# Scaled upper words of 20 weight pieces in idle PSUM banks, all scaled on ScalarE: local attention and a rational FFN on one core

## The chip, the cores and the metric

The kernel runs on one core of a Trainium2 chip. A core has five engines with an instruction stream each: TensorE (PE: matrix products and transposes; PEld is its loading of weights), VectorE (DVE), ScalarE (ACT), GpSimd (POOL) and SyncE (SP, which here issues nearly all DMAs). SBUF is the working memory with 128 partitions; PSUM has eight banks of 2 KB per partition. Products land in PSUM. GpSimd works on SBUF alone here. The metric is the device time of one launch in microseconds, the median of several runs; lower is better.

## The reference: what is computed

Attention with a window of 96 keys and 8 global keys, over 4 batches, 8 heads, 768 positions and head size 64, then an FFN with a rational activation, 512 to 2048 to 512, over the 3072 tokens. Cut to what matters:

```python
scores = scale * np.matmul(q, k.transpose(0, 1, 3, 2))
keep = is_global | is_local
scores = np.where(keep, scores + bias, -1000000000.0)
a = np.exp(scores - np.max(scores, axis=-1, keepdims=True))
x = np.matmul(a / np.sum(a), v)          # as 3072 x 512
...
h = x @ w_in                              # 512 x 2048
P = a[0] + a[1] * h + a[2] * h2 + a[3] * h3
Q = 1.0 + np.abs(b[0]) * np.abs(h) + np.abs(b[1]) * h2
return ((P / (Q + 1e-06)) @ w_out).astype(np.float32)   # 2048 x 512
```

The two weight matrices arrive as 64-bit floating-point numbers. [...]

## The kernel before

**Tiling.** The 3072 tokens are cut into 12 chunks of 256 (`TOK`). A chunk has eight attention units (two blocks of 128 positions by four pairs of heads) and eight FFN blocks of 256 hidden columns. There are 96 of each. The loop of `windowed` (L592) goes through 111 steps `t`; in each it calls the stages of several units at different ages: scores of unit t−1, transposed probabilities of t−2, values of t−3, and FFN block f, which is t−10 for the first chunks (`turn`, L588).

**What sets the order.** Each stage is given a number (`cur_priority`, from the tables `PRI` and `PRI_A` and the step), and a scheduler that simulates the engines puts every engine's instructions in a fixed order by it. On the chip an engine works through its own order strictly and waits where an operand isn't ready. Tiles are taken from pools: tiles of one tag share a fixed number of buffers, and a new one waits until an earlier one is done with.

**PSUM.** Eight banks: two with the tag `h` (the first FFN product), two `acc` (the second product's sums), one `r` (1/Q, written by ACT on L323, read and overwritten by DVE on L327 to L329), and three `t` for attention. The FFN begins about ten steps after attention, so the five banks of `h`, `acc` and `r` hold nothing in the first steps.

**The first chunk** runs with plain 32-bit products (`h` on L274, `acc` on L353) straight from the decoded weights `full`. From the second chunk on each product is a sum of three with a high and a low part of the weights (L282, L358), which `split_w` (L231) makes.

**The weights.** There are 32 pieces of 128 rows by 512 numbers, 512 KB each as they arrive: 16 of `w_in` and 16 of `w_out`. `WSCHED` says at which step which pieces are decoded, two at a time: pieces 0 and 1 at step 0, 2 and 3 at step 1, then steps 3, 4, 6, 7, 8, 9, 10 and 11 up to pieces 18 and 19, and the last 12 at steps 12 to 16. `fetch` (L175) brings a piece into one of five raw buffers by a DMA on SP (L182). `decode` (L184) then works in four steps; `MODE` lists who does the first two (3 for piece 0, 5 for pieces 1, 3, 5, 7, 9, 11, 14, 17 and 20, 2 for the other 22):

- L211 or L213: the upper words, read as a 32-bit number, times 2 to the −112, into the piece's SBUF buffer `dst`: by POOL (mode 5) or by ACT, which takes the magnitude as well.
- L215 (POOL, or ACT on L217 for the first piece): the upper half of the lower word, scaled to three bits, in place in the raw buffer (`low`).
- L218 (DVE): the sign of the upper word joined to `low`, in place in the raw buffer. It needs no scaled upper word.
- L220 (DVE): the scaled upper word shifted left by three, joined to `low`, in `dst`.

All operands of L218 and L220 lie in SBUF. The raw buffer is free for the next fetch after L220.

**Others named below.** L463 is attention's mask and row extreme on DVE, L473 the exponentials on ACT, L476 a small sum after them on DVE, L544 the first chunk's attention output; L313, L314 and L327 to L329 are the FFN's operations on DVE, L315 its addition on POOL.

Of the kernel before, what the change touches and what calls it, by code (L numbers as in the profile page):

```python
# [9 lines left out]
F32 = mybir.dt.float32  # L10
FR = mybir.dt.float32r
I32 = mybir.dt.int32
BF16 = mybir.dt.bfloat16
U16 = mybir.dt.uint16
AF = mybir.ActivationFunctionType
ALU = mybir.AluOpType
PSUM = bass.MemoryType.PSUM

P = 128
# [3 lines left out]
FLOOR = -0.5 + 2.0 ** -14  # L23
# [16 lines left out]

SPLITS = {4: 0, 5: 2, 6: 4, 7: 8, 8: 12, 9: 16, 10: 19, 11: 22, 12: 25, 13: 28, 14: 32}

MODE = (3, 5, 2, 5, 2, 5, 2, 5, 2, 5, 2, 5, 2, 2, 5, 2, 2, 5, 2, 2, 5, 2, 2, 2, 2, 2, 2, 2, 2, 2, 2, 2)
HI_V = (0, 2, 4, 6, 8, 10, 12, 14, 16, 18, 20, 22, 24, 26, 28, 30)
LO_V = (13, 15, 17, 19, 21, 23, 25, 27, 29, 31)

# [59 lines left out]
def tile_kernel(ctx: ExitStack, tc: tile.TileContext, q, k, v, n_global, n_local,  # L106
                w_in, w_out, ca, cb, out):
    nc = tc.nc
# [5 lines left out]
    TOK = 2 * P  # L114
# [8 lines left out]
    pl = SimpleNamespace(tmps=TMPS, gbufs=GBUFS, split=False)  # L123
# [34 lines left out]
    full = {}  # L158
    hi = {}

    def piece(dt, key):
        return wide.tile([P, 2 * TOK], dt, tag="w", name=f"w{'_'.join(map(str, key))}{'f' if dt is F32 else 'h'}",
                         bufs=NCT * DF // (2 * TOK) + NFT + 1)
# [11 lines left out]
    def fetch(key, eng=nc.sync):  # L175
        z, r, j = (*key, 0)[0:3]
        r = slice(r * P, (r + 1) * P)
        src = w_in_i[r, 4 * j * TOK:4 * (j + 1) * TOK] if z else w_out_i[r, :]
        home = (pl.early, "raw", 2) if (len(full) + len(fetched)) % 5 in (1, 3) else (pl.ffn, "g", pl.gbufs)
        raw = home[0].tile([P, 2, 2, TOK], F32, tag=home[1], name="r" + "_".join(map(str, key)), bufs=home[2])  # L180
        raw = fetched[key] = raw.rearrange("p z a b -> p (z a b)").rearrange("p (f w) -> p f w", w=2)
        eng.dma_start(out=raw.bitcast(I32), in_=src.rearrange("p (f w) -> p f w", w=2))  # L182

    def decode(key):  # L184
        dst = full[key] = piece(F32, key)
        if key not in fetched:
            fetch(key)
        raw = fetched.pop(key)
        bits = dst.bitcast(I32)
        top, low = raw.bitcast(I32)[:, :, 1], raw.bitcast(I32)[:, :, 0]  # L190
        half = raw.bitcast(U16).rearrange("p f (w z) -> p f w z", z=2)[:, :, 0, 1]
        mode = MODE[len(full) - 1]
        if mode < 2:


            nc.scalar.activation(out=dst, in_=raw[:, :, 1], func=AF.Abs)
            guard = nc.gpsimd if mode else nc.vector
            guard.tensor_scalar(out=dst, in0=dst, scalar1=1.125 * 2.0 ** -15, scalar2=None, op0=ALU.max)
            nc.vector.tensor_scalar(out=bits, in0=bits, scalar1=3, scalar2=0x3FFFFFFF,
                                    op0=ALU.logical_shift_left, op1=ALU.bitwise_and)  # L200
            nc.vector.scalar_tensor_tensor(out=bits, in0=top, scalar=-0x40000000, in1=bits,
                                           op0=ALU.bitwise_and, op1=ALU.bitwise_or)
            nc.vector.scalar_tensor_tensor(out=bits, in0=low, scalar=29, in1=bits,
                                           op0=ALU.logical_shift_right, op1=ALU.bitwise_or)
            return

        if mode == 5:  # L210
            nc.gpsimd.tensor_scalar(out=dst, in0=raw[:, :, 1], scalar1=2.0 ** -112, scalar2=None, op0=ALU.mult)  # L211
        else:
            nc.scalar.activation(out=dst, in_=raw[:, :, 1], func=AF.Abs, scale=2.0 ** -112)  # L213
        if mode != 3:
            nc.gpsimd.tensor_scalar(out=low, in0=half, scalar1=2.0 ** -13, scalar2=FLOOR, op0=ALU.mult, op1=ALU.add)  # L215
        else:
            nc.scalar.activation(out=low, in_=half, func=AF.Copy, scale=2.0 ** -13, bias=FLOOR)  # L217
        nc.vector.scalar_tensor_tensor(out=low, in0=top, scalar=-0x80000000, in1=low,  # L218
                                       op0=ALU.bitwise_and, op1=ALU.bitwise_or)
        nc.vector.scalar_tensor_tensor(out=bits, in0=bits, scalar=3, in1=low,  # L220
                                       op0=ALU.logical_shift_left, op1=ALU.bitwise_or)

    w_in_i = w_in.bitcast(I32)
    w_out_i = w_out.bitcast(I32)
# [333 lines left out]
    def windowed(lates):  # L558
# [33 lines left out]
        for t in range(NU + LAG + F2 + 1):  # L592
# [75 lines left out]
            for n, (kind, j) in enumerate(WSCHED.get(t, ())):  # L668
                tc.cur_priority = base + 1000 * t + pri[False]["dec"] + 50 * n
                for key in pieces(kind, j):  # L670
                    decode(key)
# [162 lines left out]
```

## Time and profile before

| what | value |
|---|---|
| median of 3 runs | 759.34 us (757.77 to 762.38) |
| the profiled execution | 762.41 us, of which the recorded span is 760.6 us |
| mean granted TensorE clock | 0.993 |
| PE busy | 730.6 us, 96% of the span |
| DVE, ACT, POOL busy | 609.0, 577.6, 455.4 us |
| DMA | 62.17 MB, mean 82 GB/s |

A busy share over the whole run says little here, because the run has a start of about 100 us, in which weights arrive and are decoded while attention is already running, and a long even part after it. In forty equal slices of the span (19 us each) the tenths of busy time are:

```profile
PE   4788989999999999999999999999999999999996
DVE  5789985888798878888788878778888788886565
ACT  5687866986887877877877877877887878776764
POOL 4585665584666666746656656566466656665441
DMA  8876500204332322323322322233322331200000
```

PE is not full in the first five slices, and DMA is at its highest there. These are the slices in which the change lies; stretches cut to fit are shown with the prediction. In such lines the engines are told apart by column, a group's row gives its count, its busy time and mean, and then the idle time of the engine just before it with what ended that.

### The profile page before, as it was taken

Reading aid. Unit: us, or ns where it says so; the run is one execution under the profiler, and the core shown is the slowest. Engines: PE = TensorE matmul, PEld = TensorE weight load, DVE = VectorE, ACT = ScalarE, POOL = GpSimd, SP = SyncE. Lnnn points to the kernel's source line nnn. Section 1 sums busy time; section 2 is a strip of 40 time slices with the busy share of each in tenths; the row PEclk is TensorE's granted clock in tenths of the full one; section 3 lists DMA queues with packets and bytes.
Section 4 is the critical chain, followed back from the end, with each engine's and each line's share of the span. In section 5 each row is a group of like instructions: output and inputs, shape, how many; then the busy total and the mean of one; then the engine's idle time right before and its main releaser. Section 6 shows DMA issues by size and latency. Waiting matters only on the chain.

```text
span 760.6 us, 15061 instructions
## 1 busy us (share of the span) xinstructions
PE 730.6 (96%) x5072; PEld 635.3 (84%) x5072; DVE 609.0 (80%) x1440; ACT 577.6 (76%) x1302; POOL 455.4 (60%) x488
## 2 busy tenths in 40 slices
PE   4788989999999999999999999999999999999996
PEld 3566657788988988998999989988988988998995
DVE  5789985888798878888788878778888788886565
ACT  5687866986887877877877877877887878776764
POOL 4585665584666666746656656566466656665441
PEclk9999999999999999999999999999999999999999
DMA  8876500204332322323322322233322331200000
GB/s 232 254 245 181 185 22 15 57 22 111 91 79 69 104 64 58 101 64 74 101 53 58 101 61 66 84 78 77 89 59 64 90 72 37 71 16 1 28 1 33
DMA packets 111959, 62.17 MB, mean 82 GB/s; under 512 B 81664, under 2 KB 100096, under 8 KB 111872
## 3 DMA queue, kind: packets, MB, share of 16 engines
q1 hardware_dynamic: 111584, 61.11, 29.8%
q8 instruction: 42, 0.69, 0.4%
q14 instruction: 45, 0.37, 0.2%
q10 hardware_dynamic: 288, 0.00, 0.0%
HBM read 35.92 MB, written 6.29 MB: 55 GB/s over the span
## 4 chain that ended last, share of the span: by engine, by line
PE 87%; DVE 6%; DMA 2%; issue 2%; POOL 1%; ACT 1%; SPq 0%; DVEq 0%; POOLq 0%
PE h L282 34%; PE acc L358 33%; PE o L522 5%; PE tp L497 5%; PE s L449 4%; PE acc L353 3%; DVE r L218 2%; DMA r<-in_moe_w_in_dram 2%; PE s L444 1%; PE tk L394 1%; PE h L274 1%; DMA nat<-in_k_dram 1%; DVE pr L463 1%; PE o L513 0%; POOL r L215 0%
## 5 line engine op out<-in xcount | busy, mean ns | idle before, releaser
L487 POOL TENSOR_SCALAR pr<-pr,stats 128x256 f32<-128x256 f32 (+1 forms) x152 | 132.9, 885 | 108.8 <-DVE stats L478 64.5
L282 PE MATMUL h<-xh,win_l 128*128 128x256 f32 x704 | 197.5, 281 | 0.0
L315 POOL TENSOR_TENSOR fa<-fa,fs 128x512 f32<-128x512 f32 x95 | 125.1, 1317 | 83.2 <-ACT fs L308 73.2
L358 PE MATMUL acc<-wout_l,g 128*128 128x512 f32 x352 | 139.4, 396 | 0.0
L282 PEld LDWEIGHTS h<-xh,win_l 128*128 128x128 f32 x704 | 133.1, 189 | 2.0 <-issue 0.5
L338 POOL TENSOR_TENSOR g<-fu,g 128x512 fp32r<-128x512 f32 x87 | 113.9, 1309 | 32.0 <-ACT g L337 25.9
L473 ACT ACTIVATE pr<-pr,stats 128x256 f32<-128x256 f32 (+1 forms) x192 | 92.7, 485 | 30.8 <-DVE stats L463 28.9
L306 ACT ACTIVATE fu<-h,coef 128x512 f32<-128x512 f32 (+1 forms) x97 | 75.1, 774 | 27.8 <-PE h L282 23.9
L327 DVE SCALAR_TENSOR_TENSOR fu<-fu,coef,q 128x512 f32<-128x512 f32 (+1 forms) x97 | 71.7, 739 | 29.9 <-ACT q L323 27.3
L322 ACT ACTIVATE fs<-fa,coef 128x512 f32<-128x512 f32 (+1 forms) x97 | 69.5, 716 | 27.6 <-POOL fa L315 25.8
L313 DVE TENSOR_TENSOR fu<-fu,h 128x512 f32<-128x512 f32 (+1 forms) x97 | 65.5, 675 | 16.8 <-ACT fs L308 16.7
L358 PEld LDWEIGHTS acc<-wout_l,g 128*128 128x128 f32 x352 | 66.4, 189 | 9.6
L314 DVE SCALAR_TENSOR_TENSOR fu<-fu,coef,h 128x512 f32<-128x512 f32 (+1 forms) x97 | 71.7, 739 | 1.9
L427 DVE SCALAR_TENSOR_TENSOR kq<-tk,kq 64x256 fp32r<-64x256 f32 x144 | 60.8, 422 | 14.7 <-ACT kq L426 10.5
L328 DVE SCALAR_TENSOR_TENSOR q<-fa,coef,q 128x512 f32<-128x512 f32 (+1 forms) x97 | 72.1, 743 | 0.0
L499 DVE COPY pT<-tp 128x512 f32<-128x512 f32 (+1 forms) x75 | 48.4, 645 | 28.0 <-PE tp L497 26.9
L426 ACT ACTIVATE kq<-tk 64x256 fp32r<-64x256 f32 x144 | 54.3, 377 | 19.2 <-DVE kq L427 13.5
L308 ACT ACTIVATE fs<-h,coef 128x512 f32<-128x512 f32 (+1 forms) x97 | 66.3, 684 | 2.0 <-DMA out_dram<-o 1.8
L329 DVE SCALAR_TENSOR_TENSOR fu<-q,fu 128x512 f32<-128x512 f32 (+1 forms) x97 | 66.1, 681 | 1.6
L337 ACT CAST g<-fu 128x512 fp32r<-128x512 f32 (+1 forms) x89 | 54.8, 615 | 15.0 <-DVE fu L329 14.6
L307 ACT ACTIVATE fa<-h,coef 128x512 f32<-128x512 f32 (+1 forms) x97 | 65.6, 676 | 0.0
L497 PE MATMUL tp<-ident,pr 128*128 128x128 f32 x352 | 57.3, 275 | 2.5 <-DVE stats L463 2.4
(253 smaller groups left out, 2049.0 us busy)
## 6 DMA issues: line engine op xcount, KB each, us to landing
mv<-nat SPq DMA_DIRECT2D x36, 256.0 KB
qT<-kq SPq DMA_DIRECT2D x144, 64.0 KB
r<-in_moe_w_in_dram SPq DMA_DIRECT2D x16, 512.0 KB
r<-in_moe_w_out_dram SPq DMA_DIRECT2D x16, 512.0 KB
nat<-in_q_dram SPq DMA_DIRECT2D x48, 128.0 KB
nat<-in_k_dram SPq DMA_DIRECT2D x48, 128.0 KB
vt<-in_v_dram SPq DMA_DIRECT2D x48, 128.0 KB
out_dram<-o SPq DMA_DIRECT2D x24, 256.0 KB
```

The costliest lines, as they stand in the source:

```text
L282: nc.tensor.matmul(out=hps[f][:, y, :], lhsT=w[:, fs], rhs=x[:, ct, :], start=(n == 0), stop=(n == 3 * NCT - 1))
L306: nc.scalar.activation(out=u, in_=h, func=AF.Identity, scale=a3, bias=a2)
L314: nc.vector.scalar_tensor_tensor(out=u, in0=u, scalar=a1, in1=h, op0=ALU.add, op1=ALU.mult)
L315: side(f).tensor_tensor(out=a, in0=a, in1=s, op=ALU.add)
L322: nc.scalar.activation(out=s, in_=a, func=AF.Ln, bias=q1)
L327: nc.vector.scalar_tensor_tensor(out=u, in0=u, scalar=a0, in1=r, op0=ALU.add, op1=ALU.mult)
L328: nc.vector.scalar_tensor_tensor(out=r, in0=a, scalar=q1, in1=r, op0=ALU.add, op1=ALU.mult)
L338: side(f).tensor_tensor(out=g[:, 1, ys], in0=u, in1=g[:, 0, ys], op=ALU.subtract)
L358: nc.tensor.matmul(out=acc, lhsT=gs[f][:, z, y, ts], rhs=w, start=(ft == 0 and n == 0), stop=(ft == NFT - 1 and n == 2))
L473: nc.scalar.activation(out=d, in_=d, func=AF.Exp, scale=-1.0, bias=st[:, x:x + 1], accum_out=st[:, 2 + 2 * x:3 + 2 * x])
L487: nc.gpsimd.tensor_scalar(out=d, in0=d, scalar1=st[:, 6 + x:7 + x], scalar2=None, op0=ALU.mult)
L497: nc.tensor.transpose(out=t_ps[:, x, w, :], in_=pr[:, x, w, :], identity=ident)
```

## The change

For every piece ACT now scales the upper word and takes its magnitude (`mag`); POOL's version is gone, and so is the table `MODE` with a branch that no piece used. The lower word is scaled by ACT for piece 0 and by POOL for all others, as before. For pieces 0 to 19 `mag` lies in a PSUM tile, whose pool `BANKS` names by a letter: `h` for pieces 0, 2, 5 and 7, `r` for 1, 6, 10, 13, 16 and 19, `a` (tag `acc`) for the ten others. For pieces 20 to 31 it lies in `dst`, as before. The two DVE operations change places and operands: the first shifts `mag` and joins `low`, in place in `mag`; the second joins the sign of the raw upper word and writes `dst`. So the first now needs ACT's result. For the first 20 pieces each of the two reads one SBUF operand and one in PSUM; for the last 12 both operands stay in SBUF.

```diff
-MODE = (3, 5, 2, 5, 2, 5, 2, 5, 2, 5, 2, 5, 2, 2, 5, 2, 2, 5, 2, 2, 5, 2, 2, 2, 2, 2, 2, 2, 2, 2, 2, 2)
+LOW_A = (0,)
+BANKS = "hrhaa" * 2 + "raa" * 3 + "r" + " " * 12
...
-        bits = dst.bitcast(I32)
+        n = len(full) - 1
...
+        mag = dst
+        if BANKS[n] != " ":
+            pool, tag = dict(h=(pl.ps_h, "h"), r=(pl.ps_r, "r"), a=(pl.ps_o, "acc"))[BANKS[n]]
+            mag = pool.tile([P, 2 * TOK], F32, tag=tag, name=f"m{n}")
+        bits = mag.bitcast(I32)
...
-        if mode == 5:
-            nc.gpsimd.tensor_scalar(out=dst, in0=raw[:, :, 1], scalar1=2.0 ** -112, scalar2=None, op0=ALU.mult)
+        nc.scalar.activation(out=mag, in_=raw[:, :, 1], func=AF.Abs, scale=2.0 ** -112)
+        if n in LOW_A:
+            nc.scalar.activation(out=low, in_=half, func=AF.Copy, scale=2.0 ** -13, bias=FLOOR)
         else:
-            nc.scalar.activation(out=dst, in_=raw[:, :, 1], func=AF.Abs, scale=2.0 ** -112)
-        if mode != 3:
             nc.gpsimd.tensor_scalar(out=low, in0=half, scalar1=2.0 ** -13, scalar2=FLOOR, op0=ALU.mult, op1=ALU.add)
-        else:
-            nc.scalar.activation(out=low, in_=half, func=AF.Copy, scale=2.0 ** -13, bias=FLOOR)
-        nc.vector.scalar_tensor_tensor(out=low, in0=top, scalar=-0x80000000, in1=low,
-                                       op0=ALU.bitwise_and, op1=ALU.bitwise_or)
         nc.vector.scalar_tensor_tensor(out=bits, in0=bits, scalar=3, in1=low,
                                        op0=ALU.logical_shift_left, op1=ALU.bitwise_or)
+        nc.vector.scalar_tensor_tensor(out=dst.bitcast(I32), in0=top, scalar=-0x80000000, in1=bits,
+                                       op0=ALU.bitwise_and, op1=ALU.bitwise_or)
```

More of the change, by code (lines that the diff above doesn't have):

```diff
@@ L188, in decode @@
         raw = fetched.pop(key)
-        bits = dst.bitcast(I32)
+        n = len(full) - 1
         top, low = raw.bitcast(I32)[:, :, 1], raw.bitcast(I32)[:, :, 0]
         half = raw.bitcast(U16).rearrange("p f (w z) -> p f w z", z=2)[:, :, 0, 1]
[L192 to L201, printed above, removed]
-                                           op0=ALU.bitwise_and, op1=ALU.bitwise_or)
-            nc.vector.scalar_tensor_tensor(out=bits, in0=low, scalar=29, in1=bits,
-                                           op0=ALU.logical_shift_right, op1=ALU.bitwise_or)
-            return
@@ L215, in decode @@
+        nc.scalar.activation(out=mag, in_=raw[:, :, 1], func=AF.Abs, scale=2.0 ** -112)
+        if n in LOW_A:
+            nc.scalar.activation(out=low, in_=half, func=AF.Copy, scale=2.0 ** -13, bias=FLOOR)
+        else:
             nc.gpsimd.tensor_scalar(out=low, in0=half, scalar1=2.0 ** -13, scalar2=FLOOR, op0=ALU.mult, op1=ALU.add)
-        else:
-            nc.scalar.activation(out=low, in_=half, func=AF.Copy, scale=2.0 ** -13, bias=FLOOR)
-        nc.vector.scalar_tensor_tensor(out=low, in0=top, scalar=-0x80000000, in1=low,
-                                       op0=ALU.bitwise_and, op1=ALU.bitwise_or)
```

## The prediction

> **What bounds the kernel now.** I read the stretches of time first, since the change touches only the first seventh of the run. Columns: stretch, length, busy time of PE, PEld, DVE, ACT and POOL with instruction counts, granted PE clock, DMA share, GB/s. The last line is the page's span.
>
> ```profile
> 0.00:20.00 20.00, 10.21 (x45) 7.48 (x45) 11.05 (x53) 10.10 (x37) 9.26 (x22) 1.00 0.85 234
> 20.00:62.00 42.00, 33.05 (x215) 25.25 (x215) 35.47 (x92) 31.69 (x96) 31.29 (x33) 0.96 0.79 246
> 62.00:97.50 35.50, 31.11 (x161) 21.39 (x159) 35.50 (x67) 26.43 (x61) 19.37 (x21) 1.00 0.54 169
> 97.50:200.00 102.50, 102.49 (x634) 81.40 (x635) 80.84 (x188) 78.72 (x183) 65.43 (x62) 0.98 0.19 46
> 200.00:740.00 540.00, 540.00 (x3953) 488.68 (x3952) 434.92 (x1022) 422.40 (x911) 326.16 (x349) 1.00 0.26 66
> span 760.6 us, 15061 instructions
> ```
>
> From 97.5 us on PE never stops. So the weight decode, which ends near 100 us, can change the time in one way only: by the moment at which PE begins its unbroken run. PE's idle time before that is 42 − 33.05 = 8.95 us in 20 to 62 and 35.5 − 31.11 = 4.39 us in 62 to 97.5, 13.3 us together, and that is the most there is to win. In the second stretch DVE is busy all 35.5 us. The chain of waits (start, length, what) says the same: DMA until 20.50, then a mixture that is mostly DVE, then PE.
>
> ```profile
> 20.50 0.40 DVE x L544
> ...
> 85.62 1.68 DVE w_10f L220
> ...
> 96.85 0.61 DVE fu L329
> 97.51 5.40 PE acc L353 x8
> ```
>
> The timeline of PE shows what it waits for at its two long gaps, and that it then runs slower for a while: the pair of products that takes 1.02 us at 86.90 takes 1.91 us at 98.65.
>
> ```profile
> 58.39 3.72 PE L274 MATMUL h<-x,w_1f 128*128 128x256 f32 x16 [2.22 <-DVE fu L314]
> ...
> 86.90 1.02 PE L353 MATMUL acc<-w_4f,fu 128*128 128x512 f32 x2
> 97.51 1.35 PE L353 MATMUL acc<-w_6f,fu 128*128 128x512 f32 x2 [2.39 <-DVE fu L329]
> 98.65 1.91 PE L353 MATMUL acc<-w_7f,fu 128*128 128x512 f32 x2
> ```
>
> Both gaps end on DVE: it is late with the FFN because it also does two operations for each of 32 weight pieces (L218, L220). So the sum below is one of DVE's time between 20 and 97.5 us.
>
> **The change, part by part.**
>
> *POOL loses the nine upper-word scalings* (L211). Two of them lie before 20 us and seven between 20 and 62; the two lines are POOL's time for L211 in these stretches.
>
> ```profile
> 0.00:20.00 20.00, 3.25 (x2) 1.00 0.85 234
> 20.00:62.00 42.00, 12.22 (x7) 0.96 0.79 246
> ```
>
> POOL, busy 31.29 of 42 us there, drops to about 19. The two before 20 us I cost at nothing: there the chain stands on DMA, whose share is 0.85 and which no edit relieves. What the other seven are worth is what DVE pays for them now. DVE's group of L218 in 20 to 62 (busy and mean, then idle before it and its releaser) holds a direct wait for POOL, and both of its decode lines run longer than their own median. The line after it is the time of L220 in 20 to 62, the last two are L218 and L220 in 62 to 104.
>
> ```profile
> L218 DVE SCALAR_TENSOR_TENSOR r<-r 128x512 int32<-128x512 int32 x16 | 12.3, 771 | 2.3 <-POOL r L215 2.3
> 20.00:62.00 42.00, 12.69 (x15) 0.96 0.79 246
> 62.00:104.00 42.00, 11.83 (x13) 0.96 0.46 143
> 62.00:104.00 42.00, 12.63 (x14) 0.96 0.46 143
> ```
>
> *DVE's operands move to PSUM for 20 pieces.* The lengths of single instructions (minimum, median, maximum in ns) separate the kinds. L218 reads two SBUF operands; L329 reads one PSUM and one SBUF operand and has plain constants, as the new second operation does; L327 and L328 have a pointer scalar besides, and L328 also writes PSUM, as the new first operation does.
>
> ```profile
> L218 DVE SCALAR_TENSOR_TENSOR r<-r x32: 674/693/1753, 10.8 to 96.2; 128x512 int32<-128x512 int32 x32
> L327 DVE SCALAR_TENSOR_TENSOR fu<-fu,coef,q x97: 479/746/750, 61.7 to 750.3; 128x512 f32<-128x512 f32 x95, 128x256 f32<-128x256 f32 x2
> L328 DVE SCALAR_TENSOR_TENSOR q<-fa,coef,q x97: 480/748/754, 62.4 to 750.7; 128x512 f32<-128x512 f32 x95, 128x256 f32<-128x256 f32 x2
> L329 DVE SCALAR_TENSOR_TENSOR fu<-q,fu x97: 424/689/694, 64.7 to 751.2; 128x512 f32<-128x512 f32 x95, 128x256 f32<-128x256 f32 x2
> ```
>
> Two things follow. First, no operation with a PSUM operand is ever stretched, in 97 cases each and with POOL busy beside them, while the all-SBUF ones reach 1753 ns. One such stretch in the timeline: DVE starts while POOL is inside a two-operand addition and ends 0.55 us after it, which is most of its own 0.69 us.
>
> ```profile
> 52.89 1.58 POOL L315 TENSOR_TENSOR fa<-fa,fs 128x512 f32<-128x512 f32 x1
> 53.27 1.75 DVE L220 SCALAR_TENSOR_TENSOR w_2f<-w_2f,r 128x512 int32<-128x512 int32 x1
> ```
>
> So the stretch goes for the 20 pieces: in 20 to 62 it is 12.3 − 16 × 0.693 = 1.2 us on L218 and 12.69 − 15 × 0.685 = 2.4 us on L220 (0.685 estimated from L218's and L329's medians), 3.6 us. It stays for the last 12 pieces, whose operations still have two SBUF operands: (11.83 + 12.63) − 27 × 0.69 = 5.8 us in 62 to 104, where 24 of the 27 operations are theirs. Second, the PSUM operand itself costs 689 − 693, nothing, by L329; by L327 it would be 746 − 693 = 53 ns on 40 operations, 2.1 us. I take nothing, since L329 has the constants of the new operations. [...]
>
> *The wait for POOL's low words* (2.3 us, five times) arises because L215 queues behind L211 on POOL. With L211 gone, L215 follows the raw data directly. I take half, 1.2 us: DVE's first operation now also needs ScalarE's magnitude, which before only the second did, so a part of the wait moves to ACT. Queued behind that wait on DVE are the mask and row-maximum operations (L463) and the FFN's, and behind these ACT and PE.
>
> *ACT gains the seven scalings in 20 to 62* (and two before). A scaling takes about 0.66 us in SBUF, and an ACT write to PSUM 0.59 (minimum, median, maximum); the third row is DVE's wait for ACT's exponentials in this stretch.
>
> ```profile
> L213 ACT ACTIVATE w_2f<-r x4: 654/664/688, 39.1 to 48.6; 128x512 f32<-128x512 f32 x4
> L323 ACT ACTIVATE q<-fs x97: 382/594/627, 59.8 to 749.9; 128x512 f32<-128x512 f32 x95, 128x256 f32<-128x256 f32 x2
> L476 DVE TENSOR_REDUCE stats<-stats 128x2 f32<-128x4 f32 x8 | 1.2, 151 | 2.7 <-ACT pr L473 2.7
> ```
>
> 7 × 0.59 = 4.1 us go into a stretch in which ACT is idle for 42 − 31.69 = 10.3 us, so it rises from 75% to 85%. Lower bound 0 (all in idle time), upper bound 4.1 us (all on the chain through the exponentials, for which DVE waits 2.7 us now). I take a quarter, 1.0 us, the share of time in which ACT is free being nearer to the first.
>
> *Bank reuse, and SP.* The five banks are unused until FFN products begin, except for the last 1/Q piece, which meets the FFN (rival C). The fetches keep SP's order and number; a fetch waits for the second DVE operation on the piece that held its buffer. That operation still reads the raw upper words, so release comes exactly as much earlier as decoding does. That is needed, as POOL already waits for data later on (us, times, longest).
>
> ```profile
> SPq L182 <- DVE w_3f L220: 8.7, 5, 5.2
> POOL r L215 <- DMA r<-in_moe_w_in_dram: 6.0, 3, 3.4
> ```
>
> Sum: 3.6 + 1.2 − 1.0 = 3.8 us less of DVE's critical time in 20 to 62. The 62 to 97.5 stretch keeps its length, because DVE has no idle time there and its 12 pieces keep their stretch, so PE's unbroken run begins about 3.8 us earlier, near 93.7. What is late next is the same thing as now, DVE in the second stretch. The profiled execution took 762.41 us with a span of 760.6, and would be 758.6 with a span of 756.8; it stands 3.07 us over the median of the three runs (759.34), so the median becomes **755.5 us**.
>
> **The rivals.**
>
> *B: the gain is hidden.* DVE is only 84% busy in 20 to 62 (35.47 of 42). If that stretch is paced by the round trip of an attention unit over PE, ACT and DVE, or by the DMA with a share of 0.79, DVE's saving becomes idle time. For it: PE, ACT and POOL are each busy 75 to 79% there and none is full. Against it: PE's gap at 58.39 ends on DVE. Time: 759.3.
>
> *E: PSUM operands cost.* If the new operations follow L327, 2.1 us come back: 757.6. For it: L328's row, the only one that writes PSUM. Against: L328 lies only 2 ns over L327, which doesn't. [...]
>
> *C: slower, through the 1/Q bank.* There is one such bank, and piece 19 (the output weights' row 7) takes it at about the moment when the first FFN block wants it. In the old trace that block's 1/Q is written at 59.82, and piece 19's last operation ends at 65.94.
>
> ```profile
> 59.82 0.58 ACT L323 ACTIVATE q<-fs 128x512 f32<-128x512 f32 x1
> 60.34 0.66 ACT L213 ACTIVATE w_7f<-r 128x512 f32<-128x512 f32 x1
> ...
> 65.26 0.68 DVE L220 SCALAR_TENSOR_TENSOR w_7f<-w_7f,r 128x512 int32<-128x512 int32 x1
> ```
>
> If piece 19 has the bank first, the FFN's first division starts up to 65.94 − 59.82 = 6.1 us late, and PE, which waits for its result, with it: 755.5 + 6.1 = 761.6, and worse if the second FFN block's 1/Q then queues too. It decides from the point at which piece 19's DVE operations end more than 3.8 us after the time when the 1/Q could have been written. Against it: those operations can be moved ahead on DVE, and if 1/Q goes first, piece 19 is not needed until 97.51.
>
> *D: more goes.* If a freer POOL also relieves the second stretch, and PE's pauses become so short that its slow products after 97.51 vanish (98.65: 1.91 for 1.02), PE could recover up to two thirds of its 13.3 us: 8.9 us, 750.4. Against: 5.8 us of stretch stay.
>
> **How the numbers follow.** Forecast 0.50 (own range 753.5 to 757.5), B 0.18, E 0.07, C 0.12, D 0.13. The range 749.5 to 762.0 takes in the forecast, B, E and the two worked-out prices of C and D; it leaves the worse half of C and some of D. About 1%, 7.6 us, is what a measurement of this kernel can tell from no change. Faster by more than that: D and a small tail of the forecast, 0.15. Slower by more: the worse half of C, 0.06. Within: 0.79.
>
> **What would show it.** Right: L211's work is absent from POOL; L218's and L220's successors stay near 0.69 us for the 20 pieces and still reach over 1.1 for the last 12; DVE's waits for POOL's low words shrink below 1 us; PE's unbroken run starts near 94 us. Wrong: PE starts at 97 or later (B), with DVE idle in 20 to 62; single operations of 0.75 us (E); ACT's first 1/Q write waiting for a weight piece (C); a changed order of work after 100 us, which I assume away.

## The result and the profile after

The changed kernel takes 764.99 us (median of 14 runs, 763.04 to 767.22), the kernel before in the same series 760.47 (14 runs): the ratio is 1.0058, 95% interval [1.0045, 1.0071]. One of the 14 runs of the kernel before took 1498 us and doesn't enter the ratio. So the change makes the kernel slower by 0.6%, 4.5 us. That is within the 1% that the prediction called no change, but the time lies above the predicted range. The profiled execution took 764.68 us with a span of 762.9.

The stretches of the prediction, for the changed kernel (stretch, length, busy time of PE, PEld, DVE, ACT, POOL, granted clock, DMA share, GB/s):

```profile
0.00:20.00 20.00, 9.79 (x44) 7.33 (x44) 10.84 (x50) 11.53 (x40) 5.20 (x20) 1.00 0.84 236
20.00:62.00 42.00, 37.14 (x240) 28.72 (x237) 34.71 (x105) 37.21 (x109) 15.68 (x28) 1.00 0.85 263
62.00:97.50 35.50, 31.46 (x148) 20.23 (x146) 34.35 (x62) 25.65 (x59) 19.44 (x20) 0.90 0.50 147
97.50:200.00 102.50, 101.69 (x635) 81.01 (x634) 79.32 (x183) 78.68 (x180) 62.49 (x61) 1.00 0.19 49
200.00:740.00 540.00, 539.50 (x3938) 486.75 (x3937) 432.60 (x1021) 418.27 (x906) 323.83 (x348) 1.00 0.26 66
```

From 20 to 62 us the change does what was forecast: PE is busy for 37.14 us with 240 products instead of 33.05 with 215, POOL falls from 31.29 to 15.68. In the next line the clock drops to 0.90 and PE issues 13 fewer products than before (148 for 161). In the last line it issues 15 fewer (3938 for 3953) in a part of the run in which no weight is decoded (built as one 32-bit number from the two 32-bit words that it arrives in): a second loss, in a place that the change doesn't touch.

The new DVE operations by tile (minimum, median, maximum in ns; first and last start). Here L202 is ACT's magnitude, L206 POOL's lower word, L207 and L209 DVE's two operations; L183 is the fetch, and the lines after the decode stand 11 lower than before up to L353, which is now L342. The first and third row have a PSUM operand, the second and fourth have both in SBUF.

```profile
L207 DVE SCALAR_TENSOR_TENSOR m<-m,r x20: 678/696/714, 10.5 to 62.7; 128x512 int32<-128x512 int32 x20
L207 DVE SCALAR_TENSOR_TENSOR w_12f<-w_12f,r x1: 1785/1785/1785, 83.7 to 83.7; 128x512 int32<-128x512 int32 x1
...
L209 DVE SCALAR_TENSOR_TENSOR w_2f<-r,m x5: 678/686/711, 39.0 to 52.0; 128x512 int32<-128x512 int32 x5
L209 DVE SCALAR_TENSOR_TENSOR w_3f<-r,w_3f x4: 680/1046/1203, 69.8 to 78.2; 128x512 int32<-128x512 int32 x4
```

Of these operations none with a PSUM operand reaches 0.72 us (the longest takes 714 ns), and those in SBUF still reach 1.79 (1785 ns). The stretch is gone for the first 20 pieces, the PSUM operand costs nothing (a median of 696 ns for the first operation, where the old one, from SBUF, had 693), and the stretch stays for the last 12: three of the prediction's steps.

The same operation's group from 20 to 62 us gives its waits:

```profile
L207 DVE SCALAR_TENSOR_TENSOR m<-m,r 128x512 int32<-128x512 int32 x15 | 10.5, 697 | 2.9 <-POOL r L206 1.2 <-ACT m L202 1.1 <-issue 0.6
```

POOL's part fell from 2.3 to 1.2 us and a wait for ACT of 1.1 appeared, against forecasts of half and 1.0. The first FFN sums start 3.75 us earlier: at 67.36 us in the profile of before, the first line, and at 63.61 in the changed kernel's timeline of PE, from which the second fence is taken. (Three more profiles with before's order in the start, n8, n5 and b_again below, have them at 66.12, 67.80 and 67.85.)

```profile
67.36 1.02 PE L353 MATMUL acc<-w_0f,fu 128*128 128x512 f32 x2
```

```profile
63.61 1.12 PE L342 MATMUL acc<-w_0f,fu 128*128 128x512 f32 x2
...
72.58 1.11 PE L486 MATMUL tp<-ident,pr 128*128 128x128 f32 x4 [2.60 <-ACT kF L404]
74.57 2.05 PE L433 MATMUL s<-kF,qz 128*128 128x256 f32 x4 [0.87 <-ACT pT L488]
...
76.83 1.92 PE L342 MATMUL acc<-w_2f,fu 128*128 128x512 f32 x2
...
98.46 1.13 PE L342 MATMUL acc<-w_6f,fu 128*128 128x512 f32 x2 [0.81 <-DVE fu L318]
```

Then PE pauses for 2.60 and 0.87 us, and products run slower for a while, at a granted clock of 0.50 from 72.45 to 79.28 us: the pair at 76.83 takes 1.92 us where the one at 63.61 takes 1.12. PE's last pause of the start ends at 98.46, not near 93.7 as forecast and not at 97.51 as before.

The chain of waits (start, length, what) leads into the pause:

```profile
64.29 3.78 DMA r<-in_moe_w_in_dram
...
68.25 0.89 POOL r L206
69.14 0.08 issue
69.22 1.28 POOL fa L304
70.50 0.02 issue
70.52 0.72 ACT fs L311
...
72.26 0.27 ACT kF L404
```

A weight piece's data come at 68.1 us. POOL's lower word of that piece stands ahead of the FFN's addition (L304) in POOL's order, so the addition waits; behind it waits ACT, and behind ACT's L311 stands the copy of the keys (L404) that PE needs. My first reading went one link further back. ACT's magnitude of piece 19 wants the one 1/Q bank (tag `r`), and the FFN's first block holds that bank until DVE's L318 ends at 61.97:

```profile
61.30 0.67 DVE L318 SCALAR_TENSOR_TENSOR fu<-q,fu 128x512 f32<-128x512 f32 x1
...
63.47 0.69 DVE L209 SCALAR_TENSOR_TENSOR w_7f<-r,m 128x512 int32<-128x512 int32 x1
```

ACT's magnitude starts at 62.00, and piece 19's last operation ends at 64.16, 0.13 us before the fetch at 64.29. ACT shows no idle time before 62.00, so this wait stands in the order that the scheduler made, not in an engine that stands still. That is rival C's bank in the other form: 1/Q had it first and the weight piece waited. Whether it is what costs the time was left to the runs.

### The profile page after: what moved, and what is told of

It is laid out like the page before. It is cut to its first block, busy times and chain, and to the rows that moved or that the text cites. A ratio compares the mean times of both kernels' runs of the same rounds, so it can differ in the third digit from the quotient of the medians.

```text
span 762.9 us, 15086 instructions
## 1 busy us (share of the span) xinstructions
PE 735.3 (96%) x5072; PEld 636.7 (83%) x5072; DVE 603.3 (79%) x1440; ACT 581.6 (76%) x1311; POOL 431.0 (57%) x479
## 4 chain that ended last, share of the span: by engine, by line
PE 87%; DVE 4%; ACT 2%; DMA 2%; issue 1%; POOL 0%; SPq 0%; POOLq 0%; DVEq 0%; ACTq 0%
PE h L271 33%; PE acc L347 32%; PE o L511 5%; PE tp L486 4%; PE s L438 4%; PE acc L342 2%; PE s L433 2%; PE h L263 1%; PE tk L383 1%; DMA r<-in_moe_w_in_dram 1%; DMA r<-in_moe_w_out_dram 1%; PE o L502 0%; ACT pr L462 0%; DVE m L207 0%; DVE pr L452 0%
## 5 line engine op out<-in xcount | busy, mean ns | idle before, releaser
L304 POOL TENSOR_TENSOR fa<-fa,fs 128x512 f32<-128x512 f32 x95 | 124.0, 1305 | 92.7 <-ACT fs L297 85.7
L311 ACT ACTIVATE fs<-fa,coef 128x512 f32<-128x512 f32 (+1 forms) x97 | 69.6, 717 | 35.1 <-POOL fa L304 33.8
L318 DVE SCALAR_TENSOR_TENSOR fu<-q,fu 128x512 f32<-128x512 f32 (+1 forms) x97 | 66.0, 681 | 1.4
```

The costliest lines, as they stand in the source:

```text
L304: side(f).tensor_tensor(out=a, in0=a, in1=s, op=ALU.add)
L311: nc.scalar.activation(out=s, in_=a, func=AF.Ln, bias=q1)
```

## The experiments

Theories. **Bank:** piece 19's wait for the 1/Q bank makes the pause near 72 us, and so the loss. **Order:** the scheduler, which simulates the engines, puts later instructions in another order when the start shifts, and the new order is slower for the rest of the run. **Decode early:** DVE's saved time goes to decoding pieces sooner, while FFN work that PE needs waits.

Ratios are to the kernel before, run on the same chip.

| label | changed from | edit | us | ratio [95% interval] |
|---|---|---|---|---|
| e1_p19 | after | piece 19 in SBUF | 763.16 | 1.0042 [1.0027, 1.0058] |
| e5_p24 | after | third raw buffer, for piece 24 | 763.66 | 1.0049 [1.0030, 1.0068] |
| n5_before_cast | before | roundings 28, 29 exchanged | 760.66 | 1.0002 [0.9986, 1.0018] |
| a7_after_cast | after | roundings 24, 25 exchanged | 763.07 | 1.0032 [1.0017, 1.0047] |
| e6_after_order_before | after | roundings 30, 31 exchanged | 761.18 | 1.0006 [0.9989, 1.0023] |
| n8_before_order_after | before | low parts 30, 31 exchanged | 765.49 | 1.0064 [1.0039, 1.0089] |
| e7_sbuf_order_before | e6 | no piece in PSUM | 759.11 | 0.9989 [0.9973, 1.0006] |
| e8_act_order_before | before | ACT scales all, roundings 30, 31 | 759.98 | 1.0003 [0.9985, 1.0022] |
| b_again | before | none | 760.64 | 1.0009 [0.9990, 1.0027] |
| e9_after_late_decode | after | last 6 pieces a step later | 762.60 | 1.0031 [1.0014, 1.0048] |
| e10_sbuf_late_decode | e9 | no piece in PSUM | 761.18 | 1.0017 [1.0002, 1.0032] |
| e11_before_late_decode | before | last 6 pieces a step later | 762.80 | 1.0028 [1.0011, 1.0045] |
| e12_p19_acc | after | piece 19 in an `acc` bank | 757.99 | 0.9962 [0.9948, 0.9976] |
| e13_p19_h | after | piece 19 in an `h` bank, roundings 24, 25 | 765.30 | 1.0057 [1.0035, 1.0079] |
| e14_only_p19 | e7 | only piece 19 in PSUM, in the `r` bank | 758.37 | 0.9961 [0.9947, 0.9975] |
| e15_sbuf_again | e7 | none | 759.64 | 0.9989 [0.9970, 1.0008] |

### First attempts: single links of the chain

```diff
-BANKS = "hrhaa" * 2 + "raa" * 3 + "r" + " " * 12
+BANKS = "hrhaa" * 2 + "raa" * 3 + " " * 13
```

> The changed kernel, with the magnitude of piece 19 alone back in SBUF, so that it does not wait for the one 1/Q bank. Theory 1 (piece 19 gets that bank only when the first FFN block is done with it, near 62 us; its raw buffer is freed at 64.2, piece 24 is fetched into it and lands at 68.1, GpSimd's order has that piece ahead of an FFN addition, and PE stands still near 70 us): the pauses of PE between 69 and 75 us (2.60 and 0.87 us) shrink below 1 us together, TensorE's clock stays at 1.00 from 70 to 80, PE's unbroken run begins near 94 us in place of 98.5, and the time falls by 3 to 5 us, to about 760. Rival (ScalarE with 9 more operations, or the DMA, paces the stretch, whichever bank is used): the pauses stay above 2.5 us, and the time stays within 1.5 us of 765. Theory 2 (much of the loss comes after 140 us, from another order of the instructions, which any edit shifts by some us): the first 100 us gain as theory 1 says, but the end time moves by something between -6 and +2 us that the first 100 us do not tell.

Measured: 763.16 us, 1.0042 for the changed kernel's 1.0058, still above before. POOL's addition no longer waits behind a lower word, but PE pauses for 1.91 us near 71 and 2.13 near 84 instead. So the bank theory is half met, and most of the loss is elsewhere: from 186 us on DVE's order in e1 is the changed kernel's, and by the reckoning of the next section e1 is level with the kernel before at 180 us (−0.1 us against b_again) and 2.8 us behind it at the end.

```diff
-home = (pl.early, "raw", 2) if (len(full) + len(fetched)) % 5 in (1, 3) else ...
+home = (pl.early, "raw", 3) if (len(full) + len(fetched)) % 5 in (1, 3) or len(full) == 25 else ...
```

> The changed kernel with a third raw buffer of the early kind, into which piece 24 is fetched, so that piece 24 does not wait for the buffer of piece 19; piece 19 keeps the 1/Q bank. Theory 1 says the raw buffer is the link between the bank and PE's pause: the fetch of piece 24 is issued before 61 us in place of 64.29, GpSimd's low word of it starts before 66 in place of 68.25, and PE's pauses between 69 and 75 us fall from 3.5 us to below 1. The time falls by 3 to 5 us. If the bank acts through the 1/Q itself or through ScalarE, the pause stays above 2.5 us although the piece is there.

Measured: 763.66 us, no gain to tell from the one of e1, with other pauses (2.04, 1.94 and 1.34 us between 72 and 88). The edit also shifted the rest of the start, so it doesn't isolate the raw buffer; the section on the bank comes back to that link. From 194 us on e5's order is before's, and its loss lies in the start alone: by the same reckoning it is 4.2 us behind b_again at 114 us and at the end.

### The late order

The order in which an engine's instructions run can be read from two traces and laid side by side, without tile numbers and line numbers. Each trace has 1445 instructions of DVE (waits on semaphores left out). The changed kernel has only the last 59 in the order of before, from 704 us on, although its source is the same for the whole even part. (The expectation of e6 below puts the end of the difference at about 290 us; the traces don't bear that out.) Tiny edits that have no bearing on the start switch between such orders. `HI_V` and `LO_V` list which of the 32 splits of the weights into a high and a low part (in the steps up to 14) DVE does; exchanging two neighbours moves two instructions.

> The kernel before, with the rounding of one weight piece (number 28 of the high parts, near 168 us) moved from VectorE to ScalarE and number 29's from ScalarE to VectorE not at all: one operation of 0.5 us on another engine, where both have idle time. By itself it is worth less than 0.3 us. Theory 2 (the order that the scheduler makes of the even part is worth some us by chance): the first 100 us stay the same within 0.5 us, and the time moves by 1 to 4 us in either direction. Rival (the late loss belongs to the change, and orders are worth the same): the time stays within 0.7 us of the kernel before.

```diff
-HI_V = (..., 24, 26, 28, 30)
+HI_V = (..., 24, 26, 29, 30)
```

(The expectation speaks of one rounding; the edit exchanges the engines of two.) Measured: 1.0002. Its last 1060 DVE instructions, from 194 us on, are in before's order, so it changed nothing that matters and tested only that such an exchange by itself costs nothing.

> The changed kernel, with the rounding of one weight piece (number 24 of the high parts) moved from VectorE to ScalarE, an operation of about 0.5 us near 155 us. Theory 2 (chance of the order in the even part): the first 100 us stay as they are within 0.5 us, the pause of PE near 72 us included, and the time moves by 1 to 4 us in either direction. Rival (the late loss belongs to the change itself): 765 within 0.7 us.

The same kind of edit on the changed kernel (25 for 24). Measured: 1.0032; from 328 us on the order is the changed kernel's, and the pauses near 72 us stay (3.2 and 0.87). It leaves the order theory untested too. The next two switch the order:

```diff
 after to e6_after_order_before
-HI_V = (..., 26, 28, 30)
+HI_V = (..., 26, 28, 31)
 before to n8_before_order_after
-LO_V = (..., 27, 29, 31)
+LO_V = (..., 27, 29, 30)
```

> The changed kernel with the rounding of high parts 30 and 31 exchanged between VectorE and ScalarE, near 172 us. All engines have the changed kernel's order up to there; from about 190 us on the scheduler's order becomes, instruction for instruction, that of the kernel before, where the changed kernel alone differs from it up to about 290 us. Theory 2 (the loss after 150 us is that other order): PE's progress against the kernel before no longer falls behind by 4 us between 150 and 360 us but by less than 0.7, and the time falls from 765 to 761 (760 to 762), with the pause near 72 us still there. Rival (the loss belongs to the changed decode, by whatever way): 765 within 1 us.

> The converse: the kernel before, with the low parts of pieces 30 and 31 exchanged between VectorE and GpSimd, near 172 us. The decode is untouched; from about 190 us on the order is that which the changed kernel has. Theory 2: the time rises by 3 to 4 us, to about 763.5 (ratio 1.004 to 1.005), and PE falls behind between 150 and 360 us by 3 to 4 us. Rival: within 0.8 us of the kernel before.

Measured: e6, the whole change with before's late order (its last 1060 DVE instructions, from 193 us on), takes 761.18 us and can't be told from before; by the two ratios that is 0.5% less than the changed kernel, 4.0 us. n8 has before's decode and loses before's order at 169 us; it has the changed kernel's only from 344 us on (its last 755 DVE instructions), and in between an order that is neither's. It takes 765.49 us, 0.64% or 4.9 us more than before. So another late order costs, without the change, about as much as the change lost. Part of the cost is seen in the 100 us from 190 us on, one line each for before, the changed kernel, e6 and n8:

```profile
190.00:290.00 100.00, 100.00 (x740) 90.91 (x739) 83.99 (x216) 83.42 (x188) 64.70 (x76) 1.00 0.31 80
```

```profile
190.00:290.00 100.00, 99.50 (x731) 90.22 (x730) 82.16 (x211) 80.56 (x183) 63.34 (x73) 1.00 0.31 78
```

```profile
190.00:290.00 100.00, 100.00 (x743) 91.06 (x743) 83.90 (x214) 83.25 (x187) 64.12 (x75) 1.00 0.31 80
```

```profile
190.00:290.00 100.00, 99.31 (x724) 89.75 (x724) 84.06 (x213) 81.81 (x186) 64.51 (x76) 1.00 0.32 80
```

At an equal clock of 1.00 PE issues 740 and 743 products in before's order, 731 and 724 in the other: at 100 / 740 = 0.135 us each, 1.2 and 2.2 us in this stretch alone. (The count is a rough measure, as products differ in length: e12, which loses nothing there, issues 735.) One wait of PE is recorded in each of the two slower ones (us, times, longest): the first line is the changed kernel's, ending at 246.78 us, the second n8's, ending at 209.78.

```profile
PE tp L486 <- DVE stats L452: 0.5, 1, 0.5
```

```profile
PE acc L358 <- ACT g L337: 0.6, 1, 0.6
```

The rest is spread over smaller delays that the view of PE's idle time doesn't show; which instruction of the new order makes them was not settled.

To follow a loss through the run, the next table gives the time at which the same amount of TensorE work has been started, worked out from the traces with each kind of product at its median spacing, as a difference to the second profile of before (b_again; negative is ahead).

| at, in b_again (us) | before | n8 | after | e6 | e7 | e15 | e14 | e12 |
|---|---|---|---|---|---|---|---|---|
| 63.7 | -0.5 | -1.7 | -4.7 | -3.2 | -4.1 | -4.0 | -4.2 | -4.6 |
| 78.9 | +1.4 | +0.7 | +2.2 | +3.9 | -1.2 | +1.0 | +0.1 | -0.7 |
| 114.4 | +2.9 | +2.2 | +0.8 | +1.6 | -1.1 | -0.9 | -1.3 | -2.5 |
| 180.2 | +2.9 | +2.2 | +1.9 | +2.2 | -0.5 | -0.3 | -1.4 | -2.2 |
| 374.2 | +2.9 | +5.4 | +4.3 | +2.1 | -0.6 | -0.3 | -1.5 | -2.2 |
| 743.8 | +2.9 | +6.0 | +4.9 | +2.1 | -0.6 | -0.3 | -1.5 | -2.2 |

In the kernels with before's late order the difference stays the same within 0.1 us from 180 us to the end; n8 and the changed kernel lose 3.8 and 3.0 us more. The same reckoning for all kept profiles says the same. From 200 us to the end the twelve others with before's order there stay level with b_again within 0.1 us, and the five with another order fall back by 1.9 to 3.7 us (the changed kernel 2.8, e1 2.8, e13 2.6, a7 1.9, n8 3.7). The loss comes in steps: the changed kernel has most of it between 240 and 360 us and about 1 us between 680 and 700, n8 half of it between 200 and 220. And b_again shows what a single profile is worth:

> The kernel before once more, unchanged, since its profiled execution (762.41 us) lies near the upper end of its runs. All theories: ratio 1.000 within 0.002. What is asked of its profile: how far the start of PE's unbroken run and the pauses before it differ between two executions of one and the same program. If the first 100 us vary by 2 to 3 us between executions and the rest is repeated exactly, then the change's early part must be judged by medians, and not by these single traces; if they agree within 0.5 us, the early gain of 2 us that the two traces show is a real one.

Measured: 1.0009, but its profile has a span of 757.7 us where the one shown before has 760.6, with the same program. The 2.9 us arise before 115 us.

### What the parts of the change are worth, with before's order

> The changed kernel with all magnitudes in SBUF (no PSUM tiles), and the exchange of e6_after_order_before, so that its late order is that of the kernel before. Against e6 it tells what the PSUM operands alone are worth. By the prediction's sum the stretch of the first 20 pieces' operations (3.6 us, partly caused by GpSimd's scalings that are gone here too) comes back by about 1.5 us, but the 1/Q bank's wait goes: 760 to 762, the pause near 72 us below 1 us. If the bank is not what makes the pause, it stays above 2.5 us here.

```diff
-BANKS = "hrhaa" * 2 + "raa" * 3 + "r" + " " * 12
+BANKS = " " * 32
```

> The kernel before with the nine upper words scaled by ScalarE in place of GpSimd, the order of the two VectorE operations and all else as before (all in SBUF), and the exchange of e6_after_order_before; the late order is that of the kernel before. It tells what ScalarE's taking over is worth alone. By the prediction: VectorE's wait for GpSimd (2.3 us) shrinks below 1 us, ScalarE's 4.1 us more cost 1: 759 to 760.5. If ScalarE paces the stretch from 20 to 62 us, 761.5 or more.

```diff
-MODE = (3, 5, 2, 5, 2, 5, ...)
+MODE = (3, 2, 2, 2, 2, 2, ...)
```

Measured: 759.11 us (0.9989) without PSUM, 759.98 (1.0003) for before's decode with all scaling on ACT. Neither can be told from before. In e7 DVE works 37.01 us from 20 to 62, in e6 33.53: the stretch came back by about the 3.6 us of the forecast, and the kernel is 2.1 us faster all the same. So in e6 what DVE saves there isn't what the end waits for.

### Is the saved time spent on decoding early?

```diff
-13: [(1, 7)], 14: [(0, 5)], 15: [(0, 6)], 16: [(0, 7)]}
+13: [(1, 7)], 15: [(0, 5)], 16: [(0, 6)], 17: [(0, 7)]}
```

> The changed kernel with the last six pieces (26 to 31) decoded one step later each (steps 15, 16 and 17); its late order is that of the kernel before, as in e6_after_order_before. Theory 3 (VectorE's saved time was spent on decoding the last pieces sooner, which nobody needs yet, and the FFN operations for which PE waits came no earlier): VectorE's FFN operations move ahead, PE's unbroken run begins 2 to 4 us earlier than in e6 (99.2), near 96, and the time falls 2 to 4 us below e6's 761.2, to about 758.5. Rival (PE's pause near 72 us, which hangs on the bank and the raw buffer, decides): within 1 us of 761.2.

> As e9_after_late_decode, but with all magnitudes in SBUF (as e7_sbuf_order_before). Theory 3: faster than e7 (759.1) by 1 to 3 us, to about 757.5, and the fastest of all, if the bank's wait and the sooner decoding are both real costs. Rival: 759 within 0.8.

> The kernel before with the same six pieces one step later each; late order as before. It tells whether the later decoding helps without the change. Theory 3: VectorE has no saved time to give back here, so less than in e9: between 0 and 2 us below the kernel before. If it gains as much as e9 does, the later decoding is a gain of its own that has nothing to do with the change.

Measured: 762.60, 761.18 and 762.80 us, where the first two were expected near 758. In the kernel before the same shift costs 0.28% by itself. In e9, with before's late order, PE pauses for 3.15 and 1.32 us near 72 and 2.02 near 89. The theory that pieces are decoded too early falls.

### The bank, with the order held

> The changed kernel with one letter of BANKS changed: piece 19's magnitude goes to a bank of the tag acc instead of the one 1/Q bank. The order of all DVE instructions from about 190 us on is before's again, without any exchange of roundings. Bank theory (the single 1/Q bank costs about 2 us at 70 to 80 us, the late order about 4): 758 to 759.3, ratio about 0.998, no PE pause above 2.2 us near 72, and POOL's FFN addition does not wait behind piece 24's low word. Rival (the pause near 72 us comes in any case, because ScalarE and VectorE have pieces 20 to 31 to decode there, and the bank only chooses its place): 760.5 to 761.5, as with the changed kernel in before's late order (761.18).

```diff
-BANKS = "hrhaa" * 2 + "raa" * 3 + "r" + " " * 12
+BANKS = "hrhaa" * 2 + "raa" * 3 + "a" + " " * 12
```

> All magnitudes in SBUF but piece 19's, which goes to the one 1/Q bank; roundings 30 and 31 exchanged, late order as before's. Differs by one letter from the kernel with all magnitudes in SBUF (759.11 us, 0.9989 of the kernel before). Bank theory: the bank alone costs about 2 us, so 761, ratio about 1.001, with the chain raw buffer, piece 24's fetch, POOL's low word, FFN addition in front of PE's pause near 72 us. Rival (the 2.1 us between those two kernels are chance or another piece's bank): 759, ratio 0.999, the same as the kernel with all in SBUF in this job.

```diff
-BANKS = " " * 32
+BANKS = " " * 19 + "r" + " " * 12
```

> All magnitudes in SBUF with roundings 30 and 31 exchanged, once more, as the partner of the kernel with piece 19 alone in the 1/Q bank. Both theories: 759, ratio 0.997 to 1.000.

> The changed kernel with piece 19 in a bank of the tag h, which the FFN's first products use from 57 us on, and roundings 24 and 25 exchanged so that the late order is before's. Bank theory: the bank of the first products is now the one that is shared, there are two of them and the pieces before it are done, so up to 1 us may be lost: 758.5 to 760. Rival: 760.5 to 761.5.

Measured: e12 takes 757.99 us, 0.9962 [0.9948, 0.9976]: one letter of the change replaced makes it 0.4% faster than before, and by the two ratios 1% faster than the changed kernel. About half of that 1% is the late order, which in e12 is before's from 184 us on; against e6, which has it too, the letter is worth 0.44%. But e14, with piece 19 alone in the 1/Q bank, takes 758.37 and is no slower than its partner e15 (759.64) without. So the bank theory falls as a general price: the wait costs with the other 19 pieces in PSUM (e6 761.18 against e12 757.99) and doesn't without them. And with piece 19 out of that bank the other 19 in PSUM are worth some 1.7 us (e12 757.99 against e15 759.64, whose intervals just overlap), half of the forecast gain. e13 missed: its expectation says that its late order is before's, which was an error; from 240 us on its DVE instructions are in the changed kernel's. Its 765.30 us is one more case of that order, with a start that is behind as well (3.33 us of pause near 84).

e12 also answers for the raw buffer. There piece 19 has its bank earlier (ACT's magnitude at 59.71 us for 62.00) and ends at 63.30, but the fetch that follows is issued at 64.07, only 0.22 us before the changed kernel's, and its data come later, near 68.6. What differs is POOL's order, which in e12 has the FFN's addition first:

```profile
67.36 1.27 POOL L304 TENSOR_TENSOR fa<-fa,fs 128x512 f32<-128x512 f32 x1 [2.76 <-ACT fs L297]
68.81 0.90 POOL L206 TENSOR_SCALAR r<-r 128x512 int32<-128x512 uint16 x1 [0.19 <-DMA r<-in_moe_w_in_dram]
```

So the buffer that piece 19 holds isn't the link to this pause; what is left of the chain is the place of POOL's lower word in the order.

The timeline of PE between 50 and 110 us tells what the versions have in common. First e12's pauses, and e12's stretch from 70 to 80 us:

```profile
72.11 1.93 PE L342 MATMUL acc<-w_2f,fu 128*128 128x512 f32 x2 [2.40 <-DVE fu L318]
84.47 1.10 PE L433 MATMUL s<-kF,qz 128*128 128x256 f32 x4 [1.18 <-issue]
```

```profile
70.00:80.00 10.00, 7.89 (x23) 4.57 (x24) 10.00 (x20) 8.14 (x20) 5.91 (x8) 0.83 0.71 230
```

Then the pauses of e14. The first ends, as in the changed kernel, with the copy of the keys (L404) on ACT; ahead of it ACT waited 0.63 us for POOL's addition and 0.28 us for the data of a piece:

```profile
73.06 1.12 PE L486 MATMUL tp<-ident,pr 128*128 128x128 f32 x4 [2.95 <-ACT kF L404]
95.81 1.12 PE L342 MATMUL acc<-w_6f,fu 128*128 128x512 f32 x2 [0.86 <-DVE fu L318]
```

And the changed kernel's stretch from 70 to 80 us, with its clock:

```profile
70.00:80.00 10.00, 6.55 (x15) 3.95 (x16) 10.00 (x21) 8.91 (x24) 5.20 (x8) 0.66 0.77 207
```

A pause of 2 to 3 us near 72 us comes in each of them, with the bank or without, after DVE or after ACT. What differs is whether another follows at once, and how long the clock then stays at half. In b_again there is neither a pause nor half clock between 63.7 and 78.9, so the loss in that stretch can be added up. The half-clock times are the stretches of half granted clock that the trace records.

| kernel | lost 63.7 to 78.9 us, by the table above | PE's pauses there | half clock there | pauses + half of that time |
|---|---|---|---|---|
| after | 6.9 | 2.60 + 0.87 | 6.8 | 6.9 |
| e6 | 7.1 | 2.84 + 0.87 | 6.8 | 7.1 |
| e15 | 5.0 | 0.46 + 2.60 | 3.4 | 4.8 |
| e14 | 4.4 | 2.95 | 3.4 | 4.7 |
| e12 | 4.0 | 2.40 | 3.4 | 4.1 |
| e7 | 2.9 | 0.54 + 2.09 | 0 | 2.6 |

The two columns agree within 0.3 us in all six. So the gain by 64 us, 3.2 to 4.7 us in these six, is mostly given back here, by a pause and by the clock that answers it. (n8, with before's order in the start, is 1.7 us ahead of b_again at 64 us; that much is a difference between executions.) The second pause, 0.87 us with 3.4 us more of half clock (2.6 us together), separates the changed kernel and e6 from the rest. That it goes away where piece 19 leaves the bank, and also where the other 19 leave PSUM, says that it hangs on the whole order of the start; which single instruction decides was not settled.

## Why the prediction was wrong

*The sum of DVE's time: right up to 64 us.* The stretch of 3.6 us went, PSUM operands cost nothing, POOL's wait fell to half, ACT's waits rose by 1.1. The gain at the first FFN sums was 3.75 us, the forecast 3.8. So close an agreement is luck: against n8 and b_again the gain is 2.5 and 4.2 us. Rival E falls: the new first operation has a median of 696 ns where the old one, from SBUF, had 693.

*The step that failed most: "a changed order of work after 100 us, which I assume away".* From the start to 704 us the order was another, and the table shows 3 us lost behind 180 us. e6 and n8 show it from both sides: 4.0 us back with before's order, 4.9 lost with another late order alone. The step has no term in the sum. Its 3 to 4 us are near the whole of the gain that was forecast, so with everything else right the time would have come out about level with before.

*The second: "The 62 to 97.5 stretch keeps its length".* It got longer. PE's last pause ended at 98.46 us instead of 93.7, because pauses of 2.60 and 0.87 us with 6.8 us of half clock came at 70 to 80 us. The four profiles with before's order in the start have it between 96.35 and 98.61, so nothing of the 3.8 us was left at this point. Rival B had this outcome, a gain that is hidden, but put it in the stretch from 20 to 62 us, where the gain was real. The prediction said "What is late next is the same thing as now, DVE in the second stretch"; in the changed kernel it was ACT, queued behind POOL. Here the sum took DVE's time alone for the path and left out the order in which POOL and ACT serve pieces 20 to 31.

*Rival C named the bank and closed the wrong door.* It priced 1/Q waiting for the piece. The argument against, "if 1/Q goes first, piece 19 is not needed until 97.51", forgot that the piece's place in the engines' order moves with its bank (ACT's magnitude of it stands at 62.00 us for e12's 59.71) and takes the work behind it along. But C isn't shown as the cause either: e14 has that wait, and its pause, and is faster than before.

*What held of the profile's standing.* The prediction put the profiled execution 3.07 us over the median of three runs and took that off. The direction held, for the second profile of the same program came at 759.49 us. The size didn't: over 14 runs the median is 760.47, the excess 1.94, and the forecast's base 1.1 us too low. Of the 2.9 us between the two profiles one more stretch of half clock makes 1.7; the first one also has a pause of 2.01 us, ending at 75.86, where b_again has none that is recorded.

*The forecast gain.* It was 3.8 us, and e12, with one letter other, gains 0.38%, 2.9 us. That doesn't prove the sum: against e15, with no piece in PSUM, only 1.7 us of it remain, and e12 too loses 4.0 of its early 4.6 us near 72 us. The range failed because it had no term for the order.

## What to carry to other kernels

Where a scheduler orders the instructions by simulated times, a change moves the order far behind the place of the edit; compare the order of the executed instructions in both versions down to the end, and give every version a neutral variant with the old order, before the edit itself is judged. A gain early in a run counts only if the next stretch can take it: follow the same amount of TensorE work through both traces and see where the lead is lost. For a buffer shared with later work, ask of both sides what they hold while they wait.

## What the runs showed of the hardware

Some pauses of PE cost more than their length. With the changed kernel's pauses of 2.60 and 0.87 us the granted clock is at half (0.50) for 6.8 us, from 72.45 to 79.28, which costs an estimated 3.4 more, half of that time. All such stretches between 20 and 110 us in these traces last 3.4 or 6.8 us, and they begin on a fixed grid: the stretches of full clock between two of them last whole multiples of 3.413 us (71.68 us, 21 steps, in the profile of before). Whether a pause is answered goes here by where it falls on that grid. In the two profiles of the kernel before, with the same order, one has half clock at 23.2 and 98.3 us, the other only at 57.4. The pause before 58.39 and 57.20 us is the same 2.22 us in both. In b_again it lies whole in one step of the grid, 53.97 to 57.38; in the profile of before the end of a step at 57.31 cuts it into 1.14 and 1.08. b_again's products after it run slowly (5.41 us for 16), those of the profile of before don't (3.72, in the prediction's fence).

```profile
57.20 5.41 PE L274 MATMUL h<-x,w_1f 128*128 128x256 f32 x16 [2.22 <-DVE fu L314]
```

Laid on this grid, the 18 kept traces agree between 26 and 112 us. Every step at full clock in which PE, by its recorded products, was idle for 1.91 us or more is followed by half clock (20 steps), and none with 1.89 or less is (418 steps). In a step at half clock 0.99 us or more of idle time brought another one (4 steps), 0.28 or less didn't (23). By these counts the second pause of the changed kernel, only 0.87 us, costs an estimated 2.6, half of another 3.4 included: it falls into the half-clock step that the first one brought. Before 26 us, while PE starts up, the steps don't separate as cleanly (1.71 us was answered in one trace, 1.73 wasn't in another).
